# Pairs of bfloat16 columns transposed as one float32, and a third TensorE tile in every second head

## The chip, the cores and the metric

The kernel runs on one core of a Trainium2 chip. The metric is the device time of one execution in microseconds (us), the median of several runs. The core's engines work side by side, each through its own list of instructions in order: TensorE (PE in the profile, its weight loads PEld), VectorE (DVE), ScalarE (ACT), GpSimd (POOL) and SyncE (SP, which here only issues DMAs). They wait for each other through semaphores. SBUF is the on-chip memory with 128 partitions; PSUM is the memory that TensorE writes its results to.

## What is computed

One transformer block with conditioning: 2048 tokens of width 640, 32 attention heads of width 128 over cached keys and values of 2048 rows, and then a mixer with an MLP. Cut to what matters here:

```
h = layernorm(x) * (1 + ca) + sa
q = (h @ wq), split into 32 heads of [2048, 128]
scores = q @ k_cache.T * 128 ** -0.5          # [2048, 2048] a head
p = softmax(scores, axis=-1)
o = p @ v_cache                               # [2048, 128] a head
x = x + ga * (concat(o) @ wo)
x = x + gb * B(layernorm(x) * (1 + cb) + sb)  # mixer and MLP
```

The change touches the way in which p comes from rows of queries into columns of queries, as the product with v_cache needs it. Nothing in the formulas changes.

## The kernel before

The attention stage is one loop of steps `s`. A step is one tile: 128 queries of one head against all 2048 keys. A head has 16 steps, so there are 512, and a step's number in its head is `j`. Everything is written out in one order (the class `Prog` records each operation with the names it reads and writes, and puts in the semaphore waits that follow); an engine takes its operations strictly in that order.

In step `s`, in two halves of 1024 keys each:

- TensorE computes the scores of tile `s` into `Sps` (`qk`, four products of 512 columns, L301 and L15), then half of the product of probabilities and values for tile `s - 8` (`pv`, eight products in a half, L314), then one piece of the next head's queries (`q_piece`, L246) or one piece of a transpose (`t_piece`, L262), if the step has one.
- VectorE copies each half of the scores out of PSUM, scaled by a negative number, into `negS` and takes the running minimum on the way (L594).
- GpSimd joins the two minima (L604). ScalarE computes the exponential of the whole tile, 2048 columns, into `Pb`, a ring of ten bfloat16 tiles (L607).
- The tile must then be transposed in blocks of 128 x 128 into `PTs`, a ring of ten tiles, before step `s + 8` multiplies it with the values.

Two ways of transposing stand side by side. Most tiles are transposed by DMA from SBUF to SBUF (`transpose`, L231), one issue for a pair of tiles where both go that way, else for one. SyncE issues them, and on the same queue the loads of keys (L214, transposing too), values (L223) and query weights (L218), in the written order. The tiles named in `PE_STEPS` are transposed on TensorE instead (`is_pe`): 16 transposes of 128 x 128 bfloat16, in four pieces over two steps, eight blocks to one of two PSUM banks (`JB`, shared with the query pieces). A copy (`t_evac`) then brings each bank of 1024 bfloat16 columns into `PTs`: ScalarE makes it (L271), or VectorE (L273) for the second half of the tiles 2 and 3 (`by_dve`).

`kind(h)` says which tiles of a head go to TensorE: in kind 0 the tiles 3 and 10, transposed from steps 6 and 13 on; in kind 1 the tiles 2, 3 and 10, from steps 5, 7 and 14 on. Kind 1 are the heads with `h % 4 == 1`, 8 of the 32. So 72 tiles are transposed on TensorE and 440 by DMA, with 248 issues.

ScalarE also copies each finished pair of outputs from PSUM (L585) and the next head's queries (L253, four a head). GpSimd divides the outputs by the sum of the probabilities, which comes from a column of ones beside the values (`Vaug[..., 128]`), and writes them to DRAM.

Before the loop the inputs are loaded and normed, and a table `mod_bc` of conditioning rows is built. After it follow the output projection, the mixer and the MLP.

Of the kernel before, what the change touches and what calls it, by code (L numbers as in the profile page):

```python
# [8 lines left out]
BF16 = mybir.dt.bfloat16  # L9
F32 = mybir.dt.float32  # L10
# [113 lines left out]
def bass_adaLN_cond__mha_block_cached__mixer_s_mlp__prompt_kernel(  # L124
    nc, A_x, A_k_cache, A_v_cache, A_wq, A_wo, B_x, B_w1, B_w2, B_w3, B_w4, c, w_mod, out,
):
    _, SQ, D = A_x.shape
    _, H, SK, DH = A_k_cache.shape
    FF = B_w3.shape[1]
    assert DH == 128 and D % 128 == 0 and SQ % 512 == 0 and SK == 2048  # L130
    KT = D // 128
    NQT = SQ // 128
    NQC = SQ // 512
    NKT = SK // 128
# [3 lines left out]
    SCALE = float(DH) ** -0.5  # L138
# [7 lines left out]
    with ExitStack() as es:  # L146
        sb = lambda name, shape, dt: es.enter_context(nc.sbuf_tensor(name, shape, dt))
        ps = lambda name, shape, dt: es.enter_context(nc.psum_tensor(name, shape, dt))
        o_scr = nc.dram_tensor("o_scratch", [NQT // 2, 128, H, 2, DH], BF16)
        ident = sb("ident", [128, 128], BF16)  # L150
        mod_bc = sb("mod_bc", [128, 4 * D], F32)
        Sps = ps("Sps", [128, 2048], F32)
        PTp = ps("PTp", [128, 2048], BF16)
        Oaug = ps("Oaug", [128, 512], F32)
# [3 lines left out]
        if True:  # L158
            with ExitStack() as es1:
                sb1 = lambda name, shape, dt: es1.enter_context(nc.sbuf_tensor(name, shape, dt))  # L160
                RP = 10
                PVD = 8
                PE_STEPS = ({3: 6, 10: 13}, {2: 5, 3: 7, 10: 14})
                kind = lambda h: 1 if h % 4 == 1 else 0
                US = KT * (SQ + 4)
                sb1("pad", [128, 32], F32)
                ring = sb1("ring", [128, 2 * RP, SK], BF16)
                negS = sb1("negS", [128, 3, SK], F32)
                wo = sb1("wo", [128, H, D], BF16)
                kv = sb1("kv", [128, 2 * SK + 2 * NKT * 130 + 2 * KT * 128 + 2 * SQ], BF16)  # L170
                small = sb1("small", [128, 4 * NQT + 32], F32)
                hTx = sb1("hTx", [128, US], BF16)
                Of = sb1("Of", [128, 4, 2, 130], F32)
                On = sb1("On", [128, 2, 4, 128], BF16)
                mv = small[:, 0:2 * NQT].rearrange("p (t z) -> p t z", z=2)
                sd = small[:, 2 * NQT:3 * NQT]
                rstd = small[:, 3 * NQT:4 * NQT]
# [6 lines left out]
                Vaug = kv[:, o1:o2].rearrange("p (b k d) -> p b k d", b=2, k=NKT)  # L184
                wq = kv[:, o2:o3].rearrange("p (b k d) -> p b k d", b=2, k=KT)
                QT = kv[:, o3:o3 + 2 * SQ].rearrange("p (b q) -> p b q", b=2)
                Pb = ring[:, 0:RP]
                PTs = ring[:, RP:2 * RP].rearrange("p r (k q) -> p r k q", k=NKT)
                flat = ring[:].rearrange("p r s -> p (r s)")
                XO = SK  # L190
                x_sb = flat[:, XO:XO + NQT * D].rearrange("p (t d) -> p t d", t=NQT)
                WO_ = 6 * SK
# [8 lines left out]
                CO = SO + NQT * 24  # L201
# [1 line left out]
                mcol = flat[:, CO + 2 * KT:CO + 6 * KT].bitcast(F32)  # L203
                c_sb = flat[:, CO + 6 * KT:CO + 7 * KT]
                s_col = flat[:, CO + 7 * KT:CO + 8 * KT]
                assert CO + 8 * KT <= 2 * RP * SK and XO + NQT * D <= WO_ and WO_ + KT * 2 * D <= 10 * SK
                PO = PTp[:].bitcast(F32)
                JB = [Oaug[:, 0:512], QPp[:, 0:512]]
                JBb = [Oaug[:].bitcast(BF16), QPb]
                G = Prog(nc, es1, "a")  # L210
# [16 lines left out]
                is_pe = lambda g: g % NQT in PE_STEPS[kind(g // NQT)]  # L227
# [9 lines left out]
                def bank(key):  # L237
                    if key not in bank_of:
                        bank_of[key] = jbank[0] % 2
                        jbank[0] += 1  # L240
                    return bank_of[key]
# [13 lines left out]

                def t_piece(g, r, q):
                    jb = bank(("t", g, r))

                    def f(t):
                        for z in range(4 * q, 4 * q + 4):  # L260
                            kt = 8 * r + z
                            ins = t.transpose(JBb[jb][:, z * 128:(z + 1) * 128], Pb[:, g % RP, kt * 128:(kt + 1) * 128], ident[:])  # L262
                        return ins
                    G.op("tensor", f, r=[("Pb", g % RP)], w=[("J", jb)])

                def t_evac(g, r):
                    jb = bank(("t", g, r))
                    dst = PTs[:, g % RP, r * 8:(r + 1) * 8, :]
                    src = JBb[jb].rearrange("p (k q) -> p k q", k=8)
                    if not by_dve(g, r):  # L270
                        G.op("scalar", lambda a: a.copy(dst, src), r=[("J", jb)], w=[("PT", g % RP, r)])  # L271
                    else:
                        G.op("vector", lambda v: v.tensor_copy(dst, src), r=[("J", jb)], w=[("PT", g % RP, r)])  # L273

                by_dve = lambda g, r: r == 1 and g % NQT in (2, 3)
                PIECES = []
                for steps in PE_STEPS:
                    taken = [u for j in steps.values() for u in range(2 * j, 2 * j + 4)]
# [28 lines left out]
                def pv(g, half):  # L307
                    hb = (g // NQT) % 2
                    b = g % RP
                    ob = PO[:, ((g // 2) % 2) * 512 + (g % 2) * 130:]  # L310

                    def f(t):
                        for kt in range(half * 8, half * 8 + 8):
                            ins = t.matmul(ob[:, 0:129], PTs[:, b, kt, :], Vaug[:, hb, kt, 0:129],  # L314
                                           start=(kt == 0), stop=(kt == NKT - 1))
                        return ins
                    G.op("tensor", f, r=[("PT", b, half), ("V", hb), "ones"], w=[("O", (g // 2) % 2)])
# [29 lines left out]
                if H > 1:  # L347
# [1 line left out]
                    load_k(1)  # L349
                G.dma("sync", lambda e: e.dma_start(wo[:], A_wo.rearrange("(h p) n -> p h n", p=128)), "wo", w=["wo", "woz", "wo4"])  # L350

                G.op("gpsimd", lambda g: g.memset(ident[:], 0.0), w=["id0"])
                G.op("gpsimd", lambda g: g.memset(ones_f, 1.0), w=["onesf"])
                G.op("gpsimd", lambda g: g.affine_select(out=ident[:], in_=ident[:], pattern=[[-1, 128]],
                                                         compare_op=ALU.not_equal, fill=1.0, base=0, channel_multiplier=1),
                     r=["id0"], w=["ident"])
                G.op("gpsimd", lambda g: g.memset(Vaug[:, :, :, 128:130], 1.0), w=["ones"])
                G.op("scalar", lambda a: a.activation(s_col, c_sb, ACT.Silu), r=["c"], w=["scol"])
                G.op("scalar", lambda a: a.activation(c_f, c_sb, ACT.Silu), r=["c"], w=["cf"])
                for k in range(KT):  # L360
                    G.op("gpsimd", lambda g, k=k: g.tensor_scalar(out=s_bc[:, k, :], in0=ones_f, scalar1=c_f[:, k:k + 1],
                                                                  scalar2=1.0, op0=ALU.mult, op1=ALU.mult),
                         r=["onesf", "cf"] + WRK, w=[("sbc", k)])
# [32 lines left out]
                def to_hT(cc):  # L396
                    for k in range(KT):
                        b = (4, 5, 3, 4, 5)[k % 5] if cc == NQC - 1 else (cc * KT + k) % 6

                        def f(t, k=k, b=b):  # L400
                            for z in range(4):
                                ins = t.transpose(TB[b][:, z * 128:(z + 1) * 128], x_sb[:, 4 * cc + z, k * 128:(k + 1) * 128], ident[:])
                            return ins
                        G.op("tensor", f, r=["ident"] + [("xh", 4 * cc + z) for z in range(4)] + XK[cc], w=[TK[b]])
                        if k % 2 == 0:
                            G.op("scalar", lambda a, k=k, b=b: a.activation(  # L406
                                hT[:, k, cc * 512:(cc + 1) * 512], TB[b], ACT.Identity,
                                bias=mcol[:, k:k + 1], scale=mcol[:, KT + k:KT + k + 1]),
                                r=[TK[b], "mcol"] + WRK, w=[("hT", cc, k)])
                        else:  # L410
                            G.op("vector", lambda v, k=k, b=b: v.tensor_scalar(  # L411
                                out=hT[:, k, cc * 512:(cc + 1) * 512], in0=TB[b],
                                scalar1=mcol[:, KT + k:KT + k + 1], scalar2=mcol[:, k:k + 1], op0=ALU.mult, op1=ALU.add),
                                r=[TK[b], "mcol"] + WRK, w=[("hT", cc, k)])
# [137 lines left out]
                for s in range(NG + PVD + LAG):  # L552
# [33 lines left out]
                            Of[:, p % 4].rearrange("p z d -> p (z d)")[:, 0:259], PO[:, (p % 2) * 512:(p % 2) * 512 + 259]),  # L586
                            r=[("O", p % 2)], w=[("Of", p % 4)])
                    for fn, x, y in evacs:
                        if fn is q_evac or not by_dve(x, y):
                            fn(x, y)  # L590
                    for half in range(2):
                        if s < NG:
                            r8 = s % 8
                            G.op("vector", lambda v, half=half, s=s, r8=r8: v.tensor_scalar(  # L594
                                out=negS[:, s % 3, half * 1024:(half + 1) * 1024],
                                in0=Sps[:, half * 1024:(half + 1) * 1024],
                                scalar1=-SCALE, scalar2=None, op0=ALU.mult, op1=ALU.min,
                                accum_out=(nm0 if half == 0 else nm1)[:, r8:r8 + 1]),
                                r=[("S", half)], w=[("negS", s % 3), ("nmh", half, r8)])
                    for fn, x, y in evacs:  # L600
                        if fn is t_evac and by_dve(x, y):
                            fn(x, y)
                    if s < NG:
                        G.op("gpsimd", lambda g, r8=r8: g.tensor_scalar(  # L604
                            out=nm[:, r8:r8 + 1], in0=nm0[:, r8:r8 + 1], scalar1=nm1[:, r8:r8 + 1], scalar2=None, op0=ALU.min),
# [304 lines left out]
```

## Time and profile before

| | |
|---|---|
| median of 3 runs | 1569.87 us (1567.64 to 1571.41) |
| profiled execution | span 1568.9 us from the first to the last instruction; the page gives no other time of it |
| PE busy | 1472.3 us (94%), 13947 instructions |
| PEld busy | 923.4 us (59%) |
| DVE busy | 1398.3 us (89%), 2471 instructions |
| ACT busy | 1275.9 us (81%), 1121 instructions |
| POOL busy | 623.0 us (40%) |
| granted TensorE clock, mean | 0.998 |
| DMA queue q1 | 311.30 MB, packets' time 100.8% of 16 engines' span |

The shares are over the whole span. The attention loop's first score evacuation starts at 35.38 us and its last ends at 1251.8 us; the rest is start and the later stages. A row of the timeline or the chain starts with the start in us and a length in us; a row of a group ends with busy time in us, the mean duration of one instruction in ns, and the idle time of the engine ahead of it. An instruction's duration includes the time until its result is written, so the next one on the engine can start before it ends. SyncE's rows are DMA issues; the time that a row lasts isn't the time of the transfer.

### The profile page before, as it was taken

The page shows a single profiled execution, that of the slowest core. Times are in us where ns is not written, and L with a number is a line of the kernel's source. Part 1 is how long each engine was busy: PE and PEld are TensorE (multiplying, and loading weights), DVE is VectorE, ACT ScalarE, POOL GpSimd, SP SyncE. Part 2 cuts the span into 40 slices and gives each one's busy share as a digit, 9 for nine tenths or more (in the row PEclk, how much of TensorE's full clock was granted, in tenths as well). Part 3 has the DMA queues.
Part 4 walks back from the last instruction along what each step waited for, and adds up shares of the span by engine and source line. Part 5 has one row for each costly group of instructions (what it writes and reads, how often), then busy time and mean ns, then how long its engine had stood idle before and what let it go on. Part 6 is the DMA issues. An engine that isn't in the chain of part 4 may idle for free.

```text
span 1568.9 us, 33553 instructions
## 1 busy us (share of the span) xinstructions
PE 1472.3 (94%) x13947; PEld 923.4 (59%) x13175; DVE 1398.3 (89%) x2471; ACT 1275.9 (81%) x1121; POOL 623.0 (40%) x1396
## 2 busy tenths in 40 slices
PE   5899999999999999999999999999999899999999
PEld 3466666666665566566656666566566655554545
DVE  6999999999999999999999999999999937667435
ACT  4999999999999999999999999999999900034230
POOL 0144444444444444444444444444444433323100
PEclk9999999999999999999999999999999999999999
DMA  9999999999999999999999999999999999725100
GB/s 298 239 221 239 237 242 237 233 241 243 237 240 233 239 232 232 240 236 235 229 237 236 233 243 249 226 242 243 235 241 237 238 246 190 157 53 144 38 22 34
DMA packets 1172828, 334.59 MB, mean 213 GB/s; under 512 B 1153280, under 2 KB 1166656, under 8 KB 1172672
## 3 DMA queue, kind: packets, MB, share of 16 engines
q1 hardware_dynamic: 1164192, 311.30, 100.8%
q0 software_dynamic: 6144, 16.79, 3.5%
q10 hardware_dynamic: 2336, 4.34, 0.8%
q8 instruction: 108, 1.77, 0.5%
q14 instruction: 48, 0.39, 0.1%
HBM read 43.48 MB, written 19.40 MB: 40 GB/s over the span
## 4 chain that ended last, share of the span: by engine, by line
ACT 40%; DVE 23%; PE 19%; DMA 9%; issue 7%; POOL 1%; POOLq 0%; DVEq 0%
ACT ring L607 32%; DVE negS L594 20%; DMA ring<-ring 8%; PE Sps L540 8%; PE Sps L847 4%; ACT ring L271 3%; ACT kv L253 2%; ACT Of L585 2%; PE QPp L798 2%; PE Oaug L798 2%; DVE ring L273 1%; PE Sps L783 1%; DVE ring L379 1%; DMA negS<-o_scratch 1%; PE PTp L314 1%
## 5 line engine op out<-in xcount | busy, mean ns | idle before, releaser
L594 DVE TENSOR_SCALAR_CACHE_REDUCE negS<-Sps 128x1024 f32<-128x1024 f32 x1024 | 1177.7, 1224 | 19.4 <-PE Sps L15 18.5
L607 ACT ACTIVATE ring<-negS,small 128x2048 bf16<-128x2048 f32 x512 | 1045.7, 2066 | 13.7 <-POOL small L604 12.5
L314 PEld LDWEIGHTS PTp<-kv,ring 128*128 128x128 bf16 x8192 | 554.1, 98 | 325.0 <-issue 69.6
L314 PE MATMUL PTp<-kv,ring 128*128 128x129 bf16 x8192 | 645.3, 220 | 25.0 <-DMA ring<-ring 23.9
L15 PE MATMUL Sps<-kv 128*128 128x512 bf16 x1024 | 387.9, 379 | 16.8 <-DVE negS L594 9.9
L604 POOL TENSOR_SCALAR small<-small 128x1 f32<-128x1 f32 x512 | 146.4, 286 | 621.8 <-DVE negS L594 621.7
L301 PE MATMUL Sps<-kv 128*128 128x512 bf16 x919 | 354.3, 386 | 27.8 <-DVE negS L594 16.5
L462 POOL TENSOR_SCALAR On<-Of,small 128x128 bf16<-128x128 f32 x512 | 191.0, 373 | 13.0
L301 PEld LDWEIGHTS Sps<-kv 128*128 128x128 bf16 x1024 | 98.1, 96 | 141.7 <-DVE negS L594 121.6
L455 POOL TENSOR_TENSOR small<-Of,small 128x4 f32<-128x4 f32 x128 | 133.1, 1040 | 8.8 <-ACT Of L585 8.7
L469 POOL DMA_DIRECT2D o_scratch<-On x128 | 103.1, 806 | 40.8 <-POOL On L462 37.2
L585 ACT COPY Of<-PTp 128x259 f32<-128x259 f32 x256 | 108.6, 424 | 13.2 <-PE PTp L314 13.2
L246 PE MATMUL Oaug<-hTx,kv 128*128 128x512 bf16 x268 | 101.9, 385 | 3.7 <-DVE hTx L411 3.7
L246 PE MATMUL QPp<-hTx,kv 128*128 128x512 bf16 x259 | 97.7, 382 | 2.6 <-ACT hTx L406 2.1
L728 ACT ACT_TABLE_LOAD x1 | 1.3, 1283 | 112.6 <-POOL hTx L746 112.6
L594 DVE DVE_READ_ACCUMULATOR negS<-Sps 128x1 f32 x1024 | 90.3, 88 | 0.0
L271 ACT COPY ring<-Oaug 128x1024 bf16<-128x1024 bf16 x72 | 77.0, 1069 | 0.0
L641 POOL TENSOR_SCALAR negS<-negS 128x1 f32<-128x1 f32 x48 | 24.2, 504 | 125.2 <-DVE negS L650 125.2
L540 PE MATMUL Sps<-wo,negS 128*128 128x128 bf16 (+1 forms) x503 | 69.9, 298 | 1.2 <-DMA negS<-o_scratch 0.8
L540 PE MATMUL Sps<-wo,hTx 128*128 128x512 bf16 (+1 forms) x502 | 69.3, 297 | 0.5
L851 DVE TENSOR_TENSOR ring<-Sps,ring 128x640 f32<-128x640 f32 x15 | 12.4, 824 | 59.5 <-PE Sps L847 59.5
L655 DVE TENSOR_TENSOR ring<-Sps,mod_bc 128x640 f32<-128x640 f32 x16 | 13.1, 821 | 53.6 <-PE Sps L540 32.9
(88 smaller groups left out, 1052.7 us busy)
## 6 DMA issues: line engine op xcount, KB each, us to landing
kv<-in_A_v_cache_dram SPq DMA_DIRECT2D x32, 512.0 KB, 5.0
o_scratch<-On POOLq DMA_DIRECT2D x128, 128.0 KB, 4.7
kv<-in_A_wq_dram SPq DMA_DIRECT2D x32, 160.0 KB, 3.2
wo<-in_A_wo_dram SPq DMA_DIRECT2D x1, 5120.0 KB, 16.5
ring<-ring SPq DMA_TRANSPOSE x248, 7.1
ring<-in_A_x_dram SPq DMA_DIRECT2D x5, 640.0 KB, 6.6
ring<-in_w_mod_dram SPq DMA_DIRECT2D x1, 3200.0 KB, 13.8
out_dram<-wo SPq DMA_DIRECT2D x15, 160.0 KB, 1.8
```

The lines of the kernel that those rows point to most:

```text
L15: return t.add_instruction(mybir.InstMatmult(name=t.bass.get_next_instruction_name(), ins=[t.lower_ap(rhs), t.lower_ap(lhsT)], outs=[t.low ...
L246: G.op("tensor", lambda t: t.matmul(JB[jb], wq[:, hb, q, :], hT[:, q, cc * 512:(cc + 1) * 512], start=(q == 0), stop=(q == KT - 1)), r=[(" ...
L271: G.op("scalar", lambda a: a.copy(dst, src), r=[("J", jb)], w=[("PT", g % RP, r)])
L301: ins = (t.matmul if c2 == 0 else partial(same_weights, t))(Sps[:, col:col + 512], QT[:, hb, j * 128:(j + 1) * 128], KTs[:, hb, col:col + ...
L314: ins = t.matmul(ob[:, 0:129], PTs[:, b, kt, :], Vaug[:, hb, kt, 0:129], start=(kt == 0), stop=(kt == NKT - 1))
L455: G.op("gpsimd", lambda g: g.tensor_tensor(out=rl[:, 4 * b:4 * b + 4], in0=Of[:].rearrange("p a z d -> p (a z) d")[:, 4 * b:4 * b + 4, 128 ...
L462: G.op("gpsimd", lambda g: g.tensor_scalar(out=On[:, b, z, :], in0=Of[:, 2 * b + z // 2, z % 2, 0:128], scalar1=rl[:, 4 * b + z:4 * b + z ...
L540: ins = t.matmul(YB[b][:, c0:c0 + cw], OTj[pr % 2][:, 2 * hh + z, :], wo[:, hh, c0:c0 + cw], start=(hh == 0), stop=(hh == H - 1))
L585: G.op("scalar", lambda a, p=p: a.copy(Of[:, p % 4].rearrange("p z d -> p (z d)")[:, 0:259], PO[:, (p % 2) * 512:(p % 2) * 512 + 259]), r= ...
L594: G.op("vector", lambda v, half=half, s=s, r8=r8: v.tensor_scalar(out=negS[:, s % 3, half * 1024:(half + 1) * 1024], in0=Sps[:, half * 102 ...
L604: G.op("gpsimd", lambda g, r8=r8: g.tensor_scalar(out=nm[:, r8:r8 + 1], in0=nm0[:, r8:r8 + 1], scalar1=nm1[:, r8:r8 + 1], scalar2=None, op ...
L607: G.op("scalar", lambda a, s=s, r8=r8: a.activation(Pb[:, s % RP, :], negS[:, s % 3, :], ACT.Exp, bias=nm[:, r8:r8 + 1], scale=-1.0), r=[( ...
```

## The change

A tile that goes to TensorE is now written by VectorE with its columns interleaved: within each 256 keys, key i of the first block of 128 and key i of the second block become neighbours (a step of two floats in `negS`). After the exponential, each such pair of bfloat16 numbers is taken as one float32, and TensorE transposes 128 x 128 float32, so that eight transposes replace sixteen; the pair stays together in the transposed tile. The piece is two float32 transposes for four bfloat16 ones. The copy out of PSUM moves 512 float32 for 1024 bfloat16 columns, and ScalarE makes all of them: `by_dve` is gone. The product with the values picks every second bfloat16 of the transposed tile (`PTr`) as its weights, for these tiles only.

Kind 1 is now every second head (`h % 2`), so 80 tiles are transposed on TensorE and 432 by DMA, with 240 issues.

A float32 identity `identf` is added; the bfloat16 identity moves into a part of the ring that is used only at the start, and `mod_bc`, `small` and a pad change their places in SBUF. The column of ones beside the values is now made from a transposed pattern of pairs, with two fills and a copy on GpSimd, one transpose and one copy on ScalarE.

```diff
-                kind = lambda h: 1 if h % 4 == 1 else 0
+                kind = lambda h: h % 2
+                identf = sb1("identf", [128, 128], F32)
+                PTr = ring[:, RP:2 * RP].rearrange("p r (k q z) -> p r k q z", k=NKT // 2, z=2)
+                IO = CO + 8 * KT
+                ident = flat[:, IO:IO + 128]
...
                 def t_piece(g, r, q):
                     jb = bank(("t", g, r))
+                    src = Pb[:, g % RP, :].bitcast(F32)
                     def f(t):
-                        for z in range(4 * q, 4 * q + 4):
-                            kt = 8 * r + z
-                            ins = t.transpose(JBb[jb][:, z * 128:(z + 1) * 128], Pb[:, g % RP, kt * 128:(kt + 1) * 128], ident[:])
+                        for z in range(2 * q, 2 * q + 2):
+                            c0 = (4 * r + z) * 128
+                            ins = t.transpose(JB[jb][:, z * 128:(z + 1) * 128], src[:, c0:c0 + 128], identf[:])
                         return ins
...
                 def t_evac(g, r):
                     jb = bank(("t", g, r))
-                    dst = PTs[:, g % RP, r * 8:(r + 1) * 8, :]
-                    src = JBb[jb].rearrange("p (k q) -> p k q", k=8)
-                    if not by_dve(g, r):
-                        G.op("scalar", lambda a: a.copy(dst, src), r=[("J", jb)], w=[("PT", g % RP, r)])
-                    else:
-                        G.op("vector", lambda v: v.tensor_copy(dst, src), r=[("J", jb)], w=[("PT", g % RP, r)])
-
-                by_dve = lambda g, r: r == 1 and g % NQT in (2, 3)
+                    dst = ring[:, RP + g % RP, r * 1024:(r + 1) * 1024].bitcast(F32)
+                    G.op("scalar", lambda a: a.copy(dst, JB[jb]), r=[("J", jb)], w=[("PT", g % RP, r)])
...
-                            ins = t.matmul(ob[:, 0:129], PTs[:, b, kt, :], Vaug[:, hb, kt, 0:129],
+                            pt = PTr[:, b, kt // 2, :, kt % 2] if is_pe(g) else PTs[:, b, kt, :]
+                            ins = t.matmul(ob[:, 0:129], pt, Vaug[:, hb, kt, 0:129],
...
-                G.op("gpsimd", lambda g: g.memset(Vaug[:, :, :, 128:130], 1.0), w=["ones"])
+                G.op("gpsimd", lambda g: g.tensor_copy(identf[:], ident), r=["ident"] + ringk(IO, IO + 128), w=["identf"])
+                half1 = flat[:, 0:256].rearrange("p (q z) -> p q z", z=2)
+                G.op("gpsimd", lambda g: g.memset(half1, 0.0), w=["h0", ("Pb", 0)])
+                G.op("gpsimd", lambda g: g.memset(half1[:, :, 0], 1.0), r=["h0"], w=["h1"])
+                G.op("tensor", lambda t: t.transpose(JB[0][:, 0:128], flat[:, 0:256].bitcast(F32), identf[:]),
+                     r=["h1", "identf"], w=[("J", 0)])
+                G.op("scalar", lambda a: a.copy(flat[:, 256:512].bitcast(F32), JB[0][:, 0:128]), r=[("J", 0)], w=["h2"])
+                G.op("gpsimd", lambda g: g.tensor_copy(
+                    Vaug[:, :, :, 128:130], flat[:, 256:384].rearrange("p (b k y z) -> p b k y z", b=2, k=NKT, z=2)[:, :, :, :, 0]),
+                    r=["h2", ("Pb", 0)], w=["ones"])
...
-                        if fn is q_evac or not by_dve(x, y):
-                            fn(x, y)
+                        fn(x, y)
                     for half in range(2):
                         if s < NG:
                             r8 = s % 8
+                            dst = negS[:, s % 3, half * 1024:(half + 1) * 1024]
+                            src = Sps[:, half * 1024:(half + 1) * 1024]
+                            if is_pe(s):
+                                dst = dst.rearrange("p (b i z) -> p b z i", b=4, z=2)
+                                src = src.rearrange("p (b z i) -> p b z i", b=4, z=2)
                             G.op("vector", lambda v, half=half, dst=dst, src=src, r8=r8: v.tensor_scalar(
                                 out=dst, in0=src, scalar1=-SCALE, scalar2=None, op0=ALU.mult, op1=ALU.min,
...
-                    for fn, x, y in evacs:
-                        if fn is t_evac and by_dve(x, y):
-                            fn(x, y)
```

More of the change, by code (lines that the diff above doesn't have):

```diff
@@ L149, in bass_adaLN_cond__mha_block_cached__mixer_s_mlp__prompt_kernel @@
         o_scr = nc.dram_tensor("o_scratch", [NQT // 2, 128, H, 2, DH], BF16)
-        ident = sb("ident", [128, 128], BF16)
-        mod_bc = sb("mod_bc", [128, 4 * D], F32)
         Sps = ps("Sps", [128, 2048], F32)
@@ L163, in bass_adaLN_cond__mha_block_cached__mixer_s_mlp__prompt_kernel @@
                 PE_STEPS = ({3: 6, 10: 13}, {2: 5, 3: 7, 10: 14})
-                kind = lambda h: 1 if h % 4 == 1 else 0
+                kind = lambda h: h % 2
                 US = KT * (SQ + 4)
-                sb1("pad", [128, 32], F32)
+                small = sb1("small", [128, 4 * NQT + 32], F32)
                 ring = sb1("ring", [128, 2 * RP, SK], BF16)
@@ L170, in bass_adaLN_cond__mha_block_cached__mixer_s_mlp__prompt_kernel @@
                 kv = sb1("kv", [128, 2 * SK + 2 * NKT * 130 + 2 * KT * 128 + 2 * SQ], BF16)
-                small = sb1("small", [128, 4 * NQT + 32], F32)
+                mod_bc = sb1("mod_bc", [128, 4 * D], F32)
                 hTx = sb1("hTx", [128, US], BF16)
@@ L205, in bass_adaLN_cond__mha_block_cached__mixer_s_mlp__prompt_kernel @@
                 s_col = flat[:, CO + 7 * KT:CO + 8 * KT]
-                assert CO + 8 * KT <= 2 * RP * SK and XO + NQT * D <= WO_ and WO_ + KT * 2 * D <= 10 * SK
+                IO = CO + 8 * KT
+                ident = flat[:, IO:IO + 128]
+                assert IO + 128 <= 2 * RP * SK and XO + NQT * D <= WO_ and WO_ + KT * 2 * D <= 10 * SK
                 PO = PTp[:].bitcast(F32)
@@ L257, in t_piece @@
                     jb = bank(("t", g, r))
+                    src = Pb[:, g % RP, :].bitcast(F32)
                     def f(t):
-                        for z in range(4 * q, 4 * q + 4):
-                            kt = 8 * r + z
-                            ins = t.transpose(JBb[jb][:, z * 128:(z + 1) * 128], Pb[:, g % RP, kt * 128:(kt + 1) * 128], ident[:])
+                        for z in range(2 * q, 2 * q + 2):
+                            c0 = (4 * r + z) * 128
+                            ins = t.transpose(JB[jb][:, z * 128:(z + 1) * 128], src[:, c0:c0 + 128], identf[:])
                         return ins
-                    G.op("tensor", f, r=[("Pb", g % RP)], w=[("J", jb)])
+                    G.op("tensor", f, r=[("Pb", g % RP), "identf"], w=[("J", jb)])
                 def t_evac(g, r):
                     jb = bank(("t", g, r))
-                    dst = PTs[:, g % RP, r * 8:(r + 1) * 8, :]
-                    src = JBb[jb].rearrange("p (k q) -> p k q", k=8)
-                    if not by_dve(g, r):
-                        G.op("scalar", lambda a: a.copy(dst, src), r=[("J", jb)], w=[("PT", g % RP, r)])
-                    else:
-                        G.op("vector", lambda v: v.tensor_copy(dst, src), r=[("J", jb)], w=[("PT", g % RP, r)])
-                by_dve = lambda g, r: r == 1 and g % NQT in (2, 3)
+                    dst = ring[:, RP + g % RP, r * 1024:(r + 1) * 1024].bitcast(F32)
+                    G.op("scalar", lambda a: a.copy(dst, JB[jb]), r=[("J", jb)], w=[("PT", g % RP, r)])
                 PIECES = []
@@ L350, in bass_adaLN_cond__mha_block_cached__mixer_s_mlp__prompt_kernel @@
                 G.dma("sync", lambda e: e.dma_start(wo[:], A_wo.rearrange("(h p) n -> p h n", p=128)), "wo", w=["wo", "woz", "wo4"])
-                G.op("gpsimd", lambda g: g.memset(ident[:], 0.0), w=["id0"])
+                G.op("gpsimd", lambda g: g.memset(ident, 0.0), w=["id0"])
                 G.op("gpsimd", lambda g: g.memset(ones_f, 1.0), w=["onesf"])
-                G.op("gpsimd", lambda g: g.affine_select(out=ident[:], in_=ident[:], pattern=[[-1, 128]],
+                G.op("gpsimd", lambda g: g.affine_select(out=ident, in_=ident, pattern=[[-1, 128]],
                                                          compare_op=ALU.not_equal, fill=1.0, base=0, channel_multiplier=1),
                      r=["id0"], w=["ident"])
-                G.op("gpsimd", lambda g: g.memset(Vaug[:, :, :, 128:130], 1.0), w=["ones"])
+                G.op("gpsimd", lambda g: g.tensor_copy(identf[:], ident), r=["ident"] + ringk(IO, IO + 128), w=["identf"])
[8 more added lines that the diff above has]
+                    r=["h2", ("Pb", 0)], w=["ones"])
                 G.op("scalar", lambda a: a.activation(s_col, c_sb, ACT.Silu), r=["c"], w=["scol"])
@@ L401, in f @@
                             for z in range(4):
-                                ins = t.transpose(TB[b][:, z * 128:(z + 1) * 128], x_sb[:, 4 * cc + z, k * 128:(k + 1) * 128], ident[:])
+                                ins = t.transpose(TB[b][:, z * 128:(z + 1) * 128], x_sb[:, 4 * cc + z, k * 128:(k + 1) * 128], ident)
                             return ins
-                        G.op("tensor", f, r=["ident"] + [("xh", 4 * cc + z) for z in range(4)] + XK[cc], w=[TK[b]])
+                        G.op("tensor", f, r=["ident"] + [("xh", 4 * cc + z) for z in range(4)] + XK[cc] + ringk(IO, IO + 128), w=[TK[b]])
                         if k % 2 == 0:
@@ L593, in bass_adaLN_cond__mha_block_cached__mixer_s_mlp__prompt_kernel @@
                             r8 = s % 8
[L594 to L597, printed above, removed]
+                            dst = negS[:, s % 3, half * 1024:(half + 1) * 1024]
[3 more added lines that the diff above has]
+                                src = src.rearrange("p (b z i) -> p b z i", b=4, z=2)
+                            G.op("vector", lambda v, half=half, dst=dst, src=src, r8=r8: v.tensor_scalar(
+                                out=dst, in0=src, scalar1=-SCALE, scalar2=None, op0=ALU.mult, op1=ALU.min,
                                 accum_out=(nm0 if half == 0 else nm1)[:, r8:r8 + 1]),
                                 r=[("S", half)], w=[("negS", s % 3), ("nmh", half, r8)])
-                    for fn, x, y in evacs:
-                        if fn is t_evac and by_dve(x, y):
-                            fn(x, y)
                     if s < NG:
```

## The prediction

> **What bounds the kernel now.** I read the stretches of the attention stage first (busy time of every engine), then the same stretches for the VectorE line that opens each step, then the chain of waits inside one head, then SyncE's queue in order of time, and last the groups by shape.
>
> The stretch below runs from head 1's first score evacuation to the last one, 31 heads. Columns: length, busy time with counts for PE, PEld, DVE, ACT, POOL, clock, DMA share, GB/s.
>
> ```profile
> 76.97:1251.84 1174.87, 1111.55 (x11438) 725.35 (x10657) 1161.49 (x2025) 1163.36 (x966) 541.77 (x1240) 1.00 1.21 237
> ```
>
> 31 heads in 1174.87 us are 37.90 us a head. DVE and ACT are busy 99% of it, PE 95% (35.86 us a head), so no engine alone explains the pace. The same view for the score evacuation alone, head by head (heads 3, 4 and 5; two instructions for each half):
>
> ```profile
> 152.00:189.23 37.23, 36.73 (x67) 1.00 1.18 240
> 189.23:227.55 38.32, 36.82 (x65) 1.00 1.22 239
> 227.55:265.37 37.82, 36.79 (x65) 1.00 1.20 238
> ```
>
> Heads 3 and 4 hold the same work (two tiles transposed on TensorE), yet head 4 takes 1.1 us more. Head 3 is VectorE's own floor, which the chain shows: a step of two evacuations starts every 2.29 us (667.93 to 670.22), and a bfloat16 tile evacuation costs 0.60.
>
> ```profile
> 663.99 0.60 DVE ring L273
> ...
> 667.93 1.97 DVE negS L594 x4
> 669.90 0.32 issue
> 670.22 1.97 DVE negS L594 x4
> ```
>
> 16 x 2.29 + 0.60 = 37.2: head 3. With two such copies it is 37.8: head 5, a three-tile head. ScalarE's pieces from the chain, each the time until the next piece can start:
>
> ```profile
> 605.39 0.90 ACT ring L271
> ...
> 608.46 3.79 ACT ring L607 x2
> 612.25 0.27 ACT Of L585
> ...
> 614.41 0.47 ACT kv L253
> ```
>
> 16 x 1.895 + 8 x 0.27 + 4 x 0.47 = 34.4 a head, plus 3 tile evacuations of 0.90 in a two-tile head (37.1) and 4 in a three-tile head (38.0).
>
> What made head 4 longer is the queue of DMA transposes. Here SyncE's rows in head 15: each starts 0.04 us after the end of the one before it.
>
> ```profile
> 603.08 21.38 SPq L231 DMA_TRANSPOSE ring<-ring  x5
> 624.50 2.26 SPq L214 DMA_TRANSPOSE kv<-in_A_k_cache_dram  x1
> 626.80 5.43 SPq L231 DMA_TRANSPOSE ring<-ring  x1
> ```
>
> The chain in the same head: the queue's transpose lands and only then the probability-value products go on.
>
> ```profile
> 632.91 6.74 DMA ring<-ring
> 639.65 0.04 issue
> 639.70 0.64 PE PTp L314 x8
> ```
>
> The load of the next keys stands in that queue once a head, behind a fixed tile, so its starts tell the queue's pace. Each row holds the loads of one stretch: count, shortest, median and longest ns, then the first and the last start.
>
> ```profile
> L214 SPq DMA_TRANSPOSE kv<-in_A_k_cache_dram x3: 2147/2378/2403, 130.5 to 207.3; - x3
> ...
> L214 SPq DMA_TRANSPOSE kv<-in_A_k_cache_dram x2: 2403/2574/2745, 207.3 to 242.9; - x2
> ...
> L214 SPq DMA_TRANSPOSE kv<-in_A_k_cache_dram x3: 1968/2547/2978, 1041.7 to 1118.7; - x3
> ...
> L214 SPq DMA_TRANSPOSE kv<-in_A_k_cache_dram x2: 2231/2389/2547, 1118.7 to 1153.7; - x2
> ```
>
> Between two loads that both stand in two-tile heads lie 14 tiles; there are 14 such intervals, the first two 76.8 together (130.5 to 207.3), the last two 77.0, all of them 38.37 in the mean. Where the second load stands in a three-tile head the interval holds 13 tiles: 35.6 first, 35.0 last, 35.84 in the mean of 7. So one tile is 2.5 us of the queue, and four heads as they stand are (3 x 38.37 + 35.84) / 4 = 37.74 a head. That is 0.5 above the two-tile heads' floor: the queue falls behind in them, catches up in the three-tile head, and sets the mean, with 0.16 lost around it.
>
> **The change part by part.**
>
> *Fewer DMA tiles.* Every second head instead of every fourth transposes three tiles on TensorE: 240 issues for 248, 432 tiles for 440. The queue's mean becomes (38.37 + 35.84) / 2 = 37.10, 0.63 less a head. The 13-tile heads now follow each 14-tile head, so the backlog has one head to grow instead of three.
>
> *VectorE* loses its tile copies (40 of 0.60) and keeps 16 x 2.29 = 36.6 in every head, if an evacuation that writes every second float costs what it costs now. No row shows such a write. Below it can't fall, since the reads from PSUM stay; above, half the rate adds another 1.145 to each (half of 2.29). Five such instructions fall on a mean head (2.5 tiles, two halves). I take 0, being nearest to a form whose read side is unchanged and which is limited to about one element in 1.1 ns already. [...]
>
> *ScalarE* copies all tile halves: 2 x 2.5 = 5 a head of 512 floats instead of 3.25 of 1024 bfloat16. Rows of that size:
>
> ```profile
> L253 ACT CAST kv<-QPp 128x512 bf16<-128x512 f32 x64 | 40.6, 634 | 2.4 <-PE QPp L246 2.4
> L451 ACT COPY mod_bc<-PTp 128x512 f32<-128x512 f32 x5 | 2.7, 579 | 1.0 <-PE PTp L448 1.0
> ```
>
> The cast occupies the engine 0.47 (chain above), and the float copy is not longer. So 34.4 + 4 x 0.47 = 36.3 in a two-tile head, + 6 x 0.47 = 37.2 in a three-tile head, mean 36.8. The upper end, 0.90 each as for the same bytes in bfloat16, would be 38.9; the L451 row excludes it. The copies stand ahead of the step's exponential; in a three-tile head four steps in a row have one, 1.895 + 0.47 + 0.14 = 2.5 against VectorE's 2.29, so ScalarE falls 0.9 us behind there. TensorE would feel it where it needs the copied bank again, two steps (4.6 us) later; the three score buffers take that up and the two-tile head, at 36.3, gives it back.
>
> *TensorE* does two float transposes where four bfloat16 ones stood, in 10 pieces a mean head for 9. Its rows in order of time, then two groups; the distance of the starts is the price of a piece:
>
> ```profile
> 702.29 0.63 PE L314 MATMUL PTp<-kv,ring 128*128 128x129 bf16 x8
> 702.76 0.38 PE L262 MATMUL QPp<-ident,ring 128*128 128x128 bf16 x4
> 702.99 0.39 PE L301 MATMUL Sps<-kv 128*128 128x512 bf16 x1
> ```
>
> ```profile
> L262 PEld LDWEIGHTS Oaug<-ident,ring 128*128 128x128 bf16 x576 | 38.5, 97 | 0.6
> ```
>
> Four transposes take 0.23 (0.057 each), eight products 0.47 (0.058 each), and the 97 ns weight loads hide behind them.
>
> Lower end: 0.057 each, 0.11 a piece. With the weight load wholly exposed (0.097 + 0.057) it is 0.31 a piece. [...] I take 0.23 a piece, between the first two, so PE goes from 35.86 to 36.1 a head and stays under the rest. It can afford 0.41: 35.86 - 9 x 0.23 + 10 x 0.41 = 37.9. [...]
>
> *The products that read a TensorE tile* now load weights with a step of two elements: 40 loads a mean head. No row shows such a load. Below: 0, the loads hidden as now. Above: every load exposed, + 0.097 x 40 = 3.9 a head. I take 0, the present rate; PE can afford 46 ns on each.
>
> *Start.* GpSimd gets four small operations, TensorE one transpose, ScalarE one copy at the head of its queue; the first SiLU and all behind it wait for that copy. Cover:
>
> ```profile
> 6.49 0.21 ACT L358 ACTIVATE ring<-ring 128x5 bf16<-128x5 bf16 x1 [4.47 <-DMA ring<-in_c_dram]
> ```
>
> ScalarE sits idle 4.47 us ahead of that SiLU, until its vector lands, and the seven added operations of 128 to 256 elements, each taken no longer than this 0.21, sum to 1.5 us. Cost 0, or 1.5 without that cover. The moved tiles and the identity in the ring change addresses; the ring slot that holds it is next written after the eighth step, long after its last reader.
>
> *Sum.* The engines allow about 36.9 (36.6 and 37.2 alternating), the queue 37.10; with the 0.16 kept, 37.26 a head, (37.90 - 37.26) x 31 = 19.8. The backlog starts empty and may grow a little before it stalls anything, worth some 1 us more. So -21. The profiled span is 1568.9, 1 us under the median of 1569.87: span 1548, time 1549.
>
> **The rivals.**
>
> *The transposes are hidden anyway.* The waits view says so: it puts 396.5 us of SyncE's time down to ScalarE's exponentials.
>
> ```profile
> SPq L231 <- ACT ring L607: 396.5, 105, 17.4
> ```
>
> Against it stands head 4 beside head 3, and key loads that hold the queue 2.0 to 3.0 us (the rows above) though they wait for no engine. Then only the engines count: (3 x 37.2 + 38.0) / 4 = 37.4 becomes 36.9, 0.5 x 31 = 15: 1555. Chance 0.09.
>
> *VectorE becomes the bound, on the other side.* The stepped write runs at a lower rate. Five a head, so it decides from (37.9 - 36.6) / 5 = 0.26 us on each; at half rate a head is 36.6 + 5 x 1.145 = 42.3, + 4.4 x 31: 1706. For it: DVE is at 99% with no cover. Against: the read side already paces it. Chance 0.12.
>
> *TensorE becomes the bound.* Float transposes above 0.20 us each, or stepped loads exposed by more than 46 ns. All loads exposed: 35.86 + 0.2 + 3.9 = 40.0 a head, + 65: 1635. [...] A mild case, 0.5 a piece, gives 38.8: 1598. Against: 97 ns loads hide behind 58 ns products today. Chance 0.17.
>
> *The change doesn't do what it says:* four queues all within 3% of each other collide and eat the gain; 1565 to 1573. Chance 0.06.
>
> **How the numbers follow.** The forecast has 0.56: 1549, its own range 1538 (engines' pace, 36.8 a head, -34, less friction) to 1557. Faster: 0.56 + 0.09 + 0.01 of the mild TensorE case. A measurement tells about 0.2%, 3 us, so same is 0.07, slower 0.27. Low end 1536: 1 in 20 below. The high end 1620 leaves out half rate on VectorE and the exposed or multi-pass TensorE cases, 0.15.
>
> **What would show it.** The stepped L594 evacuations last 1224 ns as now; ring copies on ScalarE about 0.6 us, 160 of them, none on VectorE; float transposes under 0.2 us apart; key loads 38 and 36 us apart in turn; heads of 36.6 to 37.5. The prediction is wrong if stepped evacuations or loads are longer than the plain ones by the margins above, or if heads stay at 37.9 with the queue no longer behind.

## The result and the profile after

The changed kernel takes 1552.82 us (median of 4 runs, 1550.04 to 1554.82) against 1570.64 for the kernel before on the same chip: ratio 0.9881, 95% interval 0.9856 to 0.9905, 18 us faster. 1549 was forecast.

The profiled execution took 1553.05 us, its span is 1550.8. Below the same stretch as in the prediction, from head 1's first score evacuation to the last one (columns: length, busy time of PE, PEld, DVE, ACT, POOL with counts, clock, DMA share, GB/s):

```profile
76.58:1231.18 1154.60, 1110.96 (x10942) 710.74 (x10150) 1138.92 (x1986) 1146.32 (x1020) 543.49 (x1240) 1.00 1.21 237
```

31 heads in 1154.60 us are 37.25 a head, 37.90 before. That is 20.3 us. The stage starts 0.4 us earlier at head 1, and what follows the last evacuation takes 319.6 us (1550.8 - 1231.2) where it took 317.1: the 20 us become 18. In the kernels of the experiments that last part is between 314 and 320 us long without any change to it, so I take the 2.6 for scatter.

The groups of the changed lines, shapes kept apart:

```profile
L606 DVE TENSOR_SCALAR_CACHE_REDUCE negS<-Sps 128x1024 f32<-128x1024 f32 x1024 | 1175.4, 1222 | 21.8 <-PE Sps L15 21.2
L313 PE MATMUL PTp<-kv,ring 128*128 128x129 bf16 x8192 | 645.4, 220 | 28.3 <-DMA ring<-ring 27.0
L313 PEld LDWEIGHTS PTp<-kv,ring 128*128 128x128 bf16 x8192 | 554.2, 98 | 348.2 <-issue 109.1 <-DMA ring<-ring 59.1 <-ACT ring L614 0.6
L265 PE MATMUL QPp<-identf,ring 128*128 128x128 f32 x320 | 61.7, 274 | 0.0
L272 ACT COPY ring<-QPp 128x512 f32<-128x512 f32 x80 | 53.9, 674 | 0.2 <-PE QPp L265 0.2
L265 PEld LDWEIGHTS QPp<-identf,ring 128*128 128x128 f32 x320 | 32.8, 142 | 0.4
```

The mean over all 1024 evacuations is 1222 ns; it was 1224. The 160 interleaved ones alone take 1223, the other 864 take 1222. The weight loads for the products last 98 ns as before (none over 101), though 1280 of the 8192 now step over every second element. Both new forms cost nothing here. A float32 transpose has a longer product (274 for 218) and load (142 for 97). What a piece costs is the distance of the starts:

```profile
703.09 0.63 PE L313 MATMUL PTp<-kv,ring 128*128 128x129 bf16 x8
703.56 0.39 PE L265 MATMUL Oaug<-identf,ring 128*128 128x128 f32 x2
703.78 0.38 PE L299 MATMUL Sps<-kv 128*128 128x512 bf16 x1
```

0.22 us, about as much as the four bfloat16 transposes that stood there (0.23). ScalarE's pieces on the chain, about steps 5 to 8 of a three-tile head:

```profile
536.35 1.90 ACT ring L614
538.25 0.27 ACT Of L593
538.52 0.49 ACT ring L272
539.00 1.90 ACT ring L614
540.90 0.48 ACT ring L272
```

The copy of half a tile holds the engine 0.48 us instead of 0.90. Two heads from the view of the evacuations alone, a two-tile and a three-tile one:

```profile
487.25:523.88 36.63, 36.63 (x65) 1.00 1.21 247
523.88:560.67 36.79, 36.78 (x65) 1.00 1.23 237
```

36.63 is VectorE's floor as forecast. Others are longer, up to 38.49 (the head from 261.43 on), and TensorE still waits for transposes. The waits view:

```profile
PEld PTp L313 <- DMA ring<-ring: 59.1, 69, 2.2
```

It was 55.5 in 73 waits. The queue has not stopped being late.

### The profile page after: what moved, and what is told of

It is laid out like the page before. It is cut to its first block, busy times and chain, and to the rows that moved or that the text cites. A ratio compares the mean times of both kernels' runs of the same rounds, so it can differ in the third digit from the quotient of the medians.

```text
span 1550.8 us, 32538 instructions
## 1 busy us (share of the span) xinstructions
PE 1472.3 (95%) x13447; PEld 909.8 (59%) x12664; DVE 1375.2 (89%) x2431; ACT 1259.8 (81%) x1179; POOL 625.8 (40%) x1399
## 4 chain that ended last, share of the span: by engine, by line
ACT 59%; PE 18%; DVE 10%; DMA 7%; issue 3%; POOL 2%; POOLq 0%; DVEq 0%
ACT ring L614 49%; DVE negS L606 8%; PE Sps L548 7%; DMA ring<-ring 5%; ACT ring L272 4%; PE Sps L854 4%; ACT Of L593 3%; ACT kv L255 3%; PE QPp L805 2%; PE Oaug L805 2%; DMA negS<-o_scratch 1%; PE Sps L790 1%; DVE ring L387 1%; POOL o_scratch L477 0%; DMA kv<-Of 0%
## 5 line engine op out<-in xcount | busy, mean ns | idle before, releaser
L606 DVE TENSOR_SCALAR_CACHE_REDUCE negS<-Sps 128x1024 f32<-128x1024 f32 x1024 | 1175.4, 1222 | 21.8 <-PE Sps L15 21.2
L614 ACT ACTIVATE ring<-negS,small 128x2048 bf16<-128x2048 f32 x512 | 1057.2, 2097 | 10.3 <-POOL small L611 9.2
L313 PE MATMUL PTp<-kv,ring 128*128 128x129 bf16 x8192 | 645.4, 220 | 28.3 <-DMA ring<-ring 27.0
L593 ACT COPY Of<-PTp 128x259 f32<-128x259 f32 x256 | 116.1, 454 | 15.0 <-PE PTp L313 15.0
L477 POOL DMA_DIRECT2D o_scratch<-On x128 | 103.4, 808 | 40.8 <-POOL On L470 37.2
L248 PE MATMUL Oaug<-hTx,kv 128*128 128x512 bf16 x257 | 97.0, 382 | 3.8 <-DVE hTx L419 3.8
L265 PE MATMUL QPp<-identf,ring 128*128 128x128 f32 x320 | 61.7, 274 | 0.0
```

Source lines behind the costliest of these rows:

```text
L248: G.op("tensor", lambda t: t.matmul(JB[jb], wq[:, hb, q, :], hT[:, q, cc * 512:(cc + 1) * 512], start=(q == 0), stop=(q == KT - 1)), r=[(" ...
L313: ins = t.matmul(ob[:, 0:129], pt, Vaug[:, hb, kt, 0:129], start=(kt == 0), stop=(kt == NKT - 1))
L477: G.dma("gpsimd", lambda e: e.dma_start(o_scr[jj // 2:jj // 2 + 2, :, hh].rearrange("a p z d -> p a (z d)"), On[:, b].rearrange("p (a z) d ...
L593: G.op("scalar", lambda a, p=p: a.copy(Of[:, p % 4].rearrange("p z d -> p (z d)")[:, 0:259], PO[:, (p % 2) * 512:(p % 2) * 512 + 259]), r= ...
L606: G.op("vector", lambda v, half=half, dst=dst, src=src, r8=r8: v.tensor_scalar(out=dst, in0=src, scalar1=-SCALE, scalar2=None, op0=ALU.mul ...
L614: G.op("scalar", lambda a, s=s, r8=r8: a.activation(Pb[:, s % RP, :], negS[:, s % 3, :], ACT.Exp, bias=nm[:, r8:r8 + 1], scale=-1.0), r=[( ...
```

## The experiments

The theory of the prediction: a mean head takes what the longer of two needs, the engines or the queue of DMA transposes. Its rival: the transposes are hidden and only the engines count. All times below stand against the kernel before in runs on the same chip, and a comparison with the changed kernel or with another run goes by these distances. The profiled execution is one run of several, so a mean head from it is good to some 0.1 us.

**One part each.** The third tile alone, in the kernel before (run e1):

```diff
-                kind = lambda h: 1 if h % 4 == 1 else 0
+                kind = lambda h: h % 2
```

> The kernel before, with three tiles on TensorE in every second head and nothing else changed (bfloat16 transposes, both copies as before). Theory (queue and engines, whichever is longer, sets the mean head): queue 37.10 a head as in the changed kernel, but ScalarE stays at 38.0 in three-tile heads and VectorE at 37.2 in two-tile heads, mean 37.6, with 0.16 lost 37.75; 0.15 x 31 = 5 us faster than before, about 1565. Rival 1, the queue alone sets the mean: 37.26 a head, 20 us faster, the whole gain. Rival 2, the transposes are hidden anyway: the mean of the engines rises from 37.4 to 37.6, 6 us slower than before.

Measured 1565.83 against 1569.42, ratio 0.9975 (0.9965 to 0.9985): 4 us faster, where 5 was expected. The rest of the change alone, with the third tile in every fourth head (e2):

```diff
-                kind = lambda h: h % 2
+                kind = lambda h: 1 if h % 4 == 1 else 0
```

> The changed kernel with three tiles on TensorE in every fourth head only, as before: the float32 transposes, the interleaved write and the ScalarE copies alone. Theory: the engines fall to 36.8 a head, but the queue stays at 37.74, so the head stays at 37.8 to 37.9: 0 to 3 us faster than before. Rival, the transposes are hidden anyway: 36.9 a head, 30 us faster than before and 12 faster than the changed kernel.

Measured 1557.51 against 1569.42, ratio 0.9925 (0.9913 to 0.9938): 12 us faster, between the 0 to 3 of the theory and the 30 of the rival. So both halves of the change carry something, 4 and 12, and the whole change 18.

The stretches of 31 heads, first of e1, then of e2 (evacuations only):

```profile
76.94:1245.42 1168.48, 1140.89 (x1986) 1.00 1.21 235
```

```profile
76.53:1239.04 1162.51, 1139.58 (x1986) 1.00 1.21 239
```

37.69 and 37.50 a head. In e2 the queue had the same 55 tiles in four heads as before, and yet the heads are 0.40 shorter. The 37.74 a head that the prediction took for the queue can't be its own need.

**The two ends.** Three tiles on TensorE in every head (e3), and two in every head (e4):

```diff
-                kind = lambda h: h % 2
+                kind = lambda h: 1        # e3; in e4: lambda h: 0
```

> The changed kernel with three tiles on TensorE in every head. Theory: the queue falls to 35.84 a head and no longer binds; ScalarE needs 37.2, so heads take 37.2 to 37.4, no DMA waits in the chain, within 4 us of the changed kernel (1549 to 1557). Rival, the queue is still what sets the changed kernel's heads and the engines have room: 36.6 to 36.8, 14 to 20 us faster than the changed kernel.

> The changed kernel with two tiles on TensorE in every head. Theory: the queue needs 38.37 a head with nowhere to catch up, engines 36.6; heads of 38.4 to 38.5, 37 us slower than the changed kernel, about 1590, which is 19 slower than before though every engine has less to do than there. Rival, hidden anyway: 36.6 to 36.7 a head, 18 us faster than the changed kernel.

e3: 1548.82, ratio 0.9871 (0.9855 to 0.9887), at the low end of what was expected. Three heads in a row, from the view of the evacuations:

```profile
634.62:671.95 37.33, 36.93 (x65) 1.00 1.17 231
...
671.95:709.28 37.33, 36.93 (x67) 1.00 1.18 231
...
709.28:746.60 37.32, 36.92 (x67) 1.00 1.17 227
```

These heads take 37.3 (37.27 in the mean of 31), which is ScalarE's sum (37.2), and the wait of TensorE's weight loads for transposes falls from 59.1 to 8.3 us:

```profile
PEld PTp L313 <- DMA ring<-ring: 8.3, 16, 1.5
```

e4: 1566.53, ratio 0.9981 (0.997 to 0.9993). It is 15 us slower than the changed kernel, which excludes the rival, but 37 was expected. All engines have less to do than before the change, and the time is nearly that of before. In e4 SyncE hardly pauses (the gaps of over 0.1 us between its rows add up to 1.1 us in the 28 heads from the key load of head 1 to that of head 29), so the distance of the key loads is the queue's pace at 14 tiles a head, as it runs there:

```profile
L216 SPq DMA_TRANSPOSE kv<-in_A_k_cache_dram x29: 1929/2122/2419, 131.9 to 1191.5; - x29
```

```profile
PEld PTp L313 <- DMA ring<-ring: 103.6, 109, 2.1
```

(1191.5 - 131.9) / 28 = 37.84, not 38.37. No wait for ScalarE hides in SyncE's rows: in none of the kernels e1 to e4, before or after does a row of L231 (L233) start ahead of the end of its tile's exponential. Where the queue has caught up, the wait is a gap ahead of the row. In e3 the exponential of the next pair ends at 652.97:

```profile
648.37 2.04 SPq L216 DMA_TRANSPOSE kv<-in_A_k_cache_dram  x1
653.00 4.27 SPq L233 DMA_TRANSPOSE ring<-ring  x1
```

In the kernel before such gaps add up to 8.0 us in the same 28 heads: its queue, too, is nearly always behind.

**The queue without any change to an engine.** The kernel before, with the transpose of tile 11 left out in two-tile heads (e5); that part of the output isn't computed.

```diff
-                            elif s % 2 == 1 or is_pe(s + 1):
+                            elif (s % 2 == 1 or is_pe(s + 1)) and not (j == 11 and h >= 1 and kind(h) == 0):
                                 transpose(s, 1)
```

> The kernel before, with the DMA transpose of tile 11 left out in the two-tile heads from head 1 on (23 single tiles; their products read what an earlier tile left in the ring, so that part of the output isn't the reference's). No engine has anything less to do. Theory, as it stands after the first four runs (a head takes its engines' floor, 37.2 or 38.0, and what the queue's backlog can't take up on top): the queue never stays behind, heads fall from 37.90 to 37.4 in the mean, about 15 us faster than before. Rival, the transposes are hidden and the backlog seen in the queue costs nothing: no change.

Measured 1555.42 against 1568.26, ratio 0.9916 (0.9901 to 0.9931): 13 us faster for 23 single tiles less on the queue. Two two-tile heads and a three-tile head:

```profile
750.39:787.61 37.22, 36.70 (x67) 1.00 1.18 232
787.61:824.83 37.22, 36.70 (x67) 1.00 1.17 231
824.83:862.64 37.81, 36.78 (x65) 1.00 1.10 218
```

These are VectorE's floors of the prediction (37.2 and 37.8), undisturbed. So the queue cost the kernel before about 13 us above its engines' floors, near the 0.5 a head (37.90 over 37.4, 15 us) that the prediction's own figures give.

**What TensorE can afford.** Each float32 transpose made twice (e6):

```diff
-                        for z in range(2 * q, 2 * q + 2):
+                        for z in (2 * q, 2 * q, 2 * q + 1, 2 * q + 1):
```

> The changed kernel with every float32 transpose of a tile made twice, one behind the other, so a piece costs 0.44 instead of 0.22 us on TensorE and nothing else changes. Theory: the prediction put the price that TensorE can afford at 0.41 a piece; at 0.44 its work is 38.2 a head, 0.95 above now, 30 us slower than the changed kernel (1575 to 1590), so slower than before. Rival, TensorE has idle time that the pieces can fill: under 10 us slower than the changed kernel.

Measured 1570.69, ratio 1.0014 (1.0002 to 1.0025): the whole gain is gone, and the loss against the changed kernel is 20 us, 30 was expected. A piece now takes 0.44, and heads are flat at 37.56 and 38.34:

```profile
889.24 0.60 PE L265 MATMUL Oaug<-identf,ring 128*128 128x128 f32 x4
889.68 0.38 PE L299 MATMUL Sps<-kv 128*128 128x512 bf16 x1
```

```profile
874.25:911.81 37.56, 37.10 (x63) 1.00 1.23 234
911.81:950.15 38.34, 37.46 (x67) 1.00 1.14 226
```

A float32 transpose that took twice as long would have made this change worth nothing. The prediction's border of 0.41 a piece was right to a few hundredths, though a mean head grew by 0.70 (37.25 to 37.95) and not by the 0.95 that the sum of TensorE's pieces gave.

**Where the rest lies.** VectorE takes one of the six copies in every second head of e3 (e7; the branches on `by_dve` that the kernel before had come back with it):

```diff
-                kind = lambda h: h % 2
+                kind = lambda h: 1
...
+                by_dve = lambda g, r: r == 1 and g % (2 * NQT) == 3
```

> The changed kernel with three tiles on TensorE in every head, and in every second head VectorE copies one of the six tile halves (tile 3, second half) instead of ScalarE. Theory: run e3 is bound by ScalarE alone at 37.32 a head in every head; this takes 0.47 from it in every second head and gives VectorE (36.62) 0.6 there, so the mean falls to 37.1 to 37.2, 4 to 7 us faster than e3, about 1543. Rival, VectorE's copy holds up its scores and TensorE behind it: no faster than e3 (1549) or slower.

Measured 1544.59, ratio 0.9848 (0.9829 to 0.9867), 3 us faster than e3, where 4 to 7 was expected. The intervals of the two ratios overlap, but the mean head of the profile falls too, from 37.27 to 37.05, so ScalarE was e3's bound. The copy on VectorE:

```profile
L275 DVE COPY ring<-QPp 128x512 f32<-128x512 f32 x16 | 11.0, 689 | 0.0
```

Three tiles in three heads of four (e8):

```diff
-                kind = lambda h: h % 2
+                kind = lambda h: 0 if h % 4 == 0 else 1
```

> The changed kernel with three tiles on TensorE in three heads of four. Theory: floors of 37.32 three times and 36.62 once, mean 37.15; the queue's backlog grows in one head only and is gone after the next; 37.15 to 37.2 a head, so 1547 to 1551, at or a little under the changed kernel. Rival, every two-tile head costs a stall of its own whatever stands around it, 37.87 as in e4: mean 37.46, 1557.

Measured 1542.84, ratio 0.9837 (0.9819 to 0.9855), better than the 1547 to 1551 expected: 37.07 a head, under the 37.15 that took the longer engine in each head by itself. A two-tile head among three-tile heads lets ScalarE catch up: its own sum is (3 x 37.2 + 36.3) / 4 = 37.0 in the mean. The rival's 37.46 is excluded, though some lateness is left: TensorE's weight loads wait 28.9 us for transposes, 8.3 in e3. The changed kernel with the products a step later (e9):

```diff
-                PVD = 8
+                PVD = 9
```

> The changed kernel with the product of probabilities and values nine steps behind the scores instead of eight (PVD = 9), so a DMA transpose may land 2.3 us later before TensorE waits; no engine and no queue has more or less to do. Theory: the changed kernel's heads of 37.25 stand 0.27 above the engines' floor of 36.97 (36.62 and 37.32), and that is late transposes; most of it goes, 5 to 8 us faster than the changed kernel (1545 to 1548). Rival, the 0.27 comes from the engines meeting each other, not from the transposes: no change.

Measured 1543.79 (1537.01 to 1549.21), ratio 0.9826 (0.9805 to 0.9846), 8 us faster than the changed kernel. The runs scatter more than elsewhere, and in the profiled one, the slowest, the heads are only 0.12 shorter (1151.05 us for 31) with 53.2 us of waits left:

```profile
PEld PTp L313 <- DMA ring<-ring: 53.2, 61, 2.2
```

The median speaks for lateness as a part of what the changed kernel has left; this run doesn't settle how large a part. The last kernel joins e8 with one copy on VectorE (e10):

> Run e8 (three tiles on TensorE in three heads of four) with VectorE copying the second half of tile 3 in the middle one of the three. Theory: ScalarE's floor falls by 0.47 in one head of four, VectorE's stays below it; 0.05 to 0.12 a head, 1539 to 1542. Rival: ScalarE is no longer what bounds e8, no change (1543).

Measured 1539.56, ratio 0.9814 (0.9799 to 0.9829), as expected; 12 us less than the changed kernel and the fastest here.

```profile
76.66:1223.29 1146.63, 1137.54 (x1986) 1.00 1.21 236
```

36.99 a head, 0.37 above VectorE's floor of 36.62.

## Why the prediction was right

*The time and the pace.* 21 us less were forecast and 18 measured; the 3 us between are the last part's 2.6. 37.26 a head was forecast, 37.25 found. The time alone doesn't choose between the theory and the rival "hidden anyway": 18 lies between the forecast's 21 and the rival's 15. The experiments have to.

*VectorE, interleaved write:* taken as 0, measured 0 (1223 ns with every second float written, 1222 without). The rival on VectorE falls with that row.

*Stepped weight loads:* taken as 0, measured 0 (98 ns, busy 645.4 us for 645.3 in the products).

*Float transposes:* 0.23 a piece taken, 0.22 measured. Their loads last 142 ns against 97 in bfloat16. The trace has 0.113 us from one transpose to the next, less than the load alone, so load and product overlap. The 0.31 a piece with the load wholly exposed is excluded by the same row. No run shows the several passes that the prediction's high end leaves out; in their place stands the measured 0.22 a piece.

*ScalarE:* 0.47 a copy taken, 0.48 found; 37.2 in a three-tile head, 37.3 in e3.

*Start:* 0 taken; the first score evacuation starts at 35.59 instead of 35.38.

*The queue* is the step that was mis-sized, and that the sum came out all the same was luck. The prediction had the whole gain from the queue: 0.63 a head for a quarter of a tile less, and nothing from the engines, since the queue was the longer. The runs take the two apart. With the queue's work unchanged, the float transposes and their copies bring 0.40 a head (37.90 to 37.50, e2; 12 us). The third tile brings 0.25 behind them (37.50 to 37.25; 6 us) and 0.21 alone (37.90 to 37.69, e1; 4 us). So the engines' share, put at 0, is 0.40 to 0.44, and the queue's, put at 0.63, is 0.21 to 0.25. The two errors cancel.

The 0.63 came from a tile's price of 2.5 us, and this from a choice of intervals. The prediction put three of the four distances between key loads at 38.37 (38.35 when added up again). One of the three, from a three-tile into a two-tile head, holds 14 tiles too and lasts 39.23 in the mean of 7. With it the four give (39.23 + 2 x 38.35 + 35.84) / 4 = 37.94. It could hardly be otherwise: a load comes once a head, so the mean distance is the pace of the heads, whatever sets it, and 37.74 with 0.16 lost around it was no measurement of the queue. A better price comes from e4, e2 and the changed kernel, in which SyncE hardly pauses (gaps of 1.1, 3.6 and 2.3 us in the 28 heads): 37.86, 37.50 and 37.25 a head with 14, 13.75 and 13.5 tiles. That is about 1.2 us a tile.

*The rival "hidden anyway"* is excluded by e4 and e5, and by e1, which it had 6 us slower. What it put down to the engines alone, 15 us, is near the 12 of e2.

*The signs.* Heads were to take 36.6 to 37.5 and take 36.6 to 38.5. Key loads were to come 38 and 36 apart in turn and come 38.7 and 35.9 apart.

*Open:* why less work on the engines shortens heads whose queue hardly ever pauses. The queue's need isn't a fixed one. SyncE's rows add up to 37.26 us a head in the kernel before and to 37.05 in e2, with the same issues. In the changed kernel they add up to 36.76, and in e6 to 35.53, with the same issues too, but there the queue waits for exponentials (gaps of 60 us in the 28 heads). What makes the rows longer while the queue is behind, no run shows. Nor does a run separate VectorE's share of the engines' gain from ScalarE's.

## What to carry to other kernels

Where several engines and a DMA queue run as near to each other as here (36.1 to 37.10 us a head in the prediction's sums for the changed kernel), neither the longest one nor the mean of the longest says what a change is worth; leave one transfer out, or move one operation to another engine, and read which heads fall to a flat floor. The distance of loads that come once a head is the pace of the heads; it prices a queue only where the queue never pauses, and then by runs with more and with less on it. Transposing two bfloat16 columns as one float32 left TensorE where it was here (0.22 us a piece for 0.23) and about halved the copy out of PSUM on ScalarE (0.48 for 0.90).

## What the runs showed of the hardware that was not expected

A transpose of 128 x 128 float32 comes every 0.113 us, twice the 0.055 of bfloat16, with the load (142 ns) partly behind the product. ScalarE's copy of the same bytes as 512 float32 instead of 1024 bfloat16 takes 0.48 instead of 0.90; VectorE's takes 689 ns (e7), and its 1024 bfloat16 took 690 before, with the next instruction 603 ns behind the start in both: VectorE gained nothing from the wider type out of PSUM.
